# Sign-carrying weight decode by Prelu, and one-hot steps and float16 copies on GpSimd, in a clustered attention and MLP kernel

## The chip, the cores and the metric

The kernel runs on 1 core of one Trainium2 chip. The metric is the device time of one execution in microseconds. TensorE is written PE in the profile, VectorE DVE, ScalarE ACT, GpSimd POOL and the engine whose queue issues the DMAs SP.

## The reference, cut to what matters

Queries and keys are assigned to the nearest of 16 centroids of their head; a query attends only to keys of its own cluster; the result goes through a two-layer MLP with a squared ReLU. All inputs come as float64.

```python
q_assign = np.argmax(np.einsum('bhsd,hcd->bhsc', q_n, c_n), axis=-1)
k_assign = np.argmax(np.einsum('bhsd,hcd->bhsc', k_n, c_n), axis=-1)
mask = q_assign[:, :, :, None] == k_assign[:, :, None, :]
scores = scale * np.matmul(q, k.transpose(0, 1, 3, 2))
scores = np.where(mask, scores, -1000000000.0)
attn = softmax(scores);  x = (attn @ v) as 3072 x 512
h = x @ w_in;  r = np.maximum(h, 0.0);  g = s * (r * r) + b
out = (g @ w_out).astype(np.float32)
```

The shapes are batch 4, 8 heads, 768 positions, head size 64; `w_in` is 512 x 2048, `w_out` 2048 x 512.

## The kernel before, in words

**Attention.** The work is cut into 192 units, one for each batch `b`, third of the sequence `c`, pair of heads `hp`, tile of 128 rows `t` and head of the pair `h`. For a unit, `scores` (L447) makes four products on TensorE: two of the data halves (KA, QA) and two of the halves that hold the mask (KB, QB). `maxima` (L461) takes the row maximum on VectorE (L465), `exps` (L467) the exponential on ScalarE (L475) into a float32 tile `p`. From unit `RAW = 8` on, `high` (L480) makes a float16 copy `ph` of `p`, and `low` (L487) subtracts it on GpSimd (L498), so that two float16 halves stand for one float32; one DMA transpose issued by SP (L500) turns both into `PT`. `values` (L502) multiplies with V. The first 8 units are turned on TensorE instead (L495). In `high` the copy is ScalarE's, but for the odd units from 17 to 35, which are VectorE's.

**Masks.** `prep_k` (L301) and `prep_q` (L332 on) prepare a pair of heads of K and four heads of Q for later units, in steps spread over the loop. Each ends in `onehot` (L283): from the products with the centroids in PSUM, VectorE takes the maximum (L288), compares (L289), multiplies with a falling row `rev` so that the first of equal maxima wins (L291), takes the maximum again (L292), compares (L293) and writes the result four times side by side as 0 and 32768 or their negatives (L294). A DMA transpose on SP's queue (L392 for `QB`, L342 for `KB`) turns it; the second pair of `scores` of the units that use it waits for that. Eight units share one `QB`. There are 16 K preparations and 24 Q preparations.

**Weights.** `fetch` (L189) loads 32 tiles (16 of each matrix), 512 KB of float64 each, into a `stage` pool of three buffers. A float64 is decoded into a float32 by hand. `rebase` (L201) reads the high 32-bit word as a float32: ScalarE multiplies it by 2^-112 (L203) and writes its sign as bf16 into `wsg` (L205). `narrow` (L207) shifts left by 3 (L209) and ors in the top three bits of the low word (L210), both on VectorE; the shift throws the sign away. `bound` (L213) gathers magnitudes: for `w_out` tiles ScalarE takes the absolute value with a running sum (L216), for `w_in` tiles TensorE adds the high halves of the words through a matrix of ones (L221) and VectorE takes the maximum (L222). GpSimd then multiplies the sign back (L223). When all are decoded, `wsplit` (L261) scales each tile into a float16 pair (L267 on ScalarE, L269 on VectorE).

**MLP.** 192 steps (12 row blocks, 16 slices of the hidden width). Step m stands `LAG = 21` units behind unit m: `mlp_in` (L575), ReLU and squares on ScalarE (L582 to L585), a subtraction on GpSimd (L590), `mlp_out` (L602).

**Order.** The loop at L700 writes the steps of unit i, MLP step i - 21, the preparations and two pieces of the weights' generator into one program. The framework then orders each engine's instructions by a timeline of its own at build time (L757, `schedule_with_timeline_sim=True`), after the priorities that `first_of_all` gives. On the chip each engine and SP's queue work strictly in the order that results.

## Time and profile before

| | |
|---|---|
| time, median of 3 runs | 986.11 us (985.94 to 988.25) |
| span of the profiled execution | 986.0 us |
| VectorE busy | 673.0 us (68%) |
| ScalarE busy | 726.4 us (74%) |
| GpSimd busy | 550.2 us (56%) |
| TensorE busy | 834.3 us (85%) |

The profile gives no other time of the profiled execution than its span, from the first instruction to the last; it stands 0.1 us from the median. Busy time is the time in which at least one instruction of an engine runs. A row of a group gives the line, the engine, the operation, output and inputs with their shapes, the count, the busy time, the mean of one in ns, and the idle time before them with what ended it. A row of the windows gives a stretch of the span, then the busy time and count of each engine, the granted clock of TensorE, the busy share of the DMA engines and the rate in GB/s.

### The profile page before, as it was taken

How to read it: one execution, taken by the hardware profiler on the slowest of the kernel's cores; microseconds unless marked ns; L12 is line 12 of the kernel's file. 1: busy time of each engine (PE TensorE's matmuls, PEld its weight loads, DVE VectorE, ACT ScalarE, POOL GpSimd, SP SyncE). 2: the span in 40 equal slices, each digit the busy share in tenths (PEclk: the TensorE clock that was granted, in tenths of full speed). 3: DMA queues.
4: the chain of work that ended last, by engine and by line, in shares of the span. 5: the costliest groups of instructions: out<-in, count | busy, mean ns of one | idle time of the engine just before them, and what ended most of it. 6: DMA issues, size and time to landing. Idle time of an engine off the chain costs nothing. (4 is left out here: it accounts for less than half of the span.)

```text
span 986.0 us, 22497 instructions
## 1 busy us (share of the span) xinstructions
PE 834.3 (85%) x8625; PEld 580.2 (59%) x8625; DVE 673.0 (68%) x1475; ACT 726.4 (74%) x1416; POOL 550.2 (56%) x543
## 2 busy tenths in 40 slices
PE   0568524887899999998799999997889999999997
PEld 0347312654566666765566666765666666767764
DVE  7798889989687665658787756578867567473100
ACT  4476776877578788867678877876788977789443
POOL 3125755556456576655467656655566766667322
PEclk9955566999999999999999999999999999999999
DMA  6865883687678775698888767797888676777200
GB/s 181 204 196 158 222 210 90 138 194 134 128 144 163 156 161 123 140 210 154 171 164 156 169 132 156 138 203 181 138 160 173 151 119 142 142 138 149 44 23 21
DMA packets 450299, 147.36 MB, mean 149 GB/s; under 512 B 417936, under 2 KB 446608, under 8 KB 450192
## 3 DMA queue, kind: packets, MB, share of 16 engines
q1 hardware_dynamic: 450192, 145.93, 69.7%
q8 instruction: 67, 1.10, 0.5%
q14 instruction: 40, 0.33, 0.1%
HBM read 35.69 MB, written 6.29 MB: 43 GB/s over the span
## 5 line engine op out<-in xcount | busy, mean ns | idle before, releaser
L498 POOL TENSOR_TENSOR ph<-p,ph 128x768 f16<-128x768 f32 x184 | 308.6, 1677 | 170.7 <-ACT ph L119 135.8
L575 PE MATMUL h<-x,wis 128*128 128x256 f16 x2304 | 292.0, 275 | 17.3 <-ACT r L582 12.2
L602 PE MATMUL acc<-wos,g 128*128 128x512 f16 x1152 | 295.4, 380 | 4.7 <-POOL g L590 2.9
L575 PEld LDWEIGHTS <-wis 128*128 128x128 f16 x2304 | 223.1, 98 | 74.9 <-issue 16.6
L590 POOL TENSOR_TENSOR g<-r,g 128x256 f16<-128x256 f32 x192 | 133.3, 695 | 139.7 <-ACT r L585 129.8
L465 DVE TENSOR_REDUCE ssm<-sc 128x1 f32<-128x768 f32 x192 | 180.9, 950 | 16.2 <-PE sc L456 16.0
L475 ACT ACTIVATE p<-sc,ssm,qsm 128x768 f32<-128x768 f32 x192 | 188.1, 980 | 3.9 <-DMA PT<-ph 1.8
L602 PEld LDWEIGHTS <-g 128*128 128x128 f16 x1152 | 104.1, 98 | 88.2 <-POOL g L590 6.9
L119 ACT ACTIVATE ph<-p 128x768 f16<-128x768 f32 x174 | 144.8, 832 | 11.1 <-DMA PT<-ph 10.8
L472 ACT ACTIVATE ssm<-ssm,lift,qsm 128x1 f32<-128x1 f32 x192 | 73.4, 382 | 101.9 <-DVE ssm L465 101.4
L517 PE MATMUL px<-vh,PT 128*128 128x65 f16 x1104 | 119.9, 196 | 14.5 <-DVE ksm L98 5.2
L582 ACT ACTIVATE r<-h,cf 128x256 f32<-128x256 f32 x192 | 89.1, 464 | 55.0 <-PE h L575 50.8
L518 PE MATMUL px<-vl,PT 128*128 128x64 f16 x1104 | 119.9, 193 | 0.0
L519 PE MATMUL px<-vh,PT 128*128 128x65 f16 x1104 | 119.9, 194 | 0.0
L456 PE MATMUL sc<-KA,QA 128*128 128x384 f16 x384 | 101.1, 343 | 20.2 <-ACT p L475 16.9
L518 PEld LDWEIGHTS <-PT 128*128 128x128 f16 x1104 | 103.6, 100 | 21.2 <-issue 12.8
L517 PEld LDWEIGHTS <-PT 128*128 128x128 f16 x1104 | 103.9, 98 | 17.5 <-issue 9.1
L456 PE MATMUL sc<-KB,QB 128*128 128x384 f16 x384 | 100.2, 345 | 7.8 <-DMA QB<-qb 7.7
L519 PEld LDWEIGHTS <-PT 128*128 128x128 f16 x1104 | 103.6, 98 | 3.0
L584 ACT ACTIVATE g<-r 128x256 f16<-128x256 f32 x192 | 79.5, 414 | 3.8
L585 ACT ACTIVATE r<-r 128x256 f32<-128x256 f32 x192 | 79.1, 412 | 3.3
L525 DVE TENSOR_SCALAR ssm<-px 128x2 f32<-128x2 f32 x92 | 14.2, 155 | 88.3 <-PE px L519 88.2
(153 smaller groups left out, 1090.9 us busy)
## 6 DMA issues: line engine op xcount, KB each, us to landing
wst<-in_moe_w_in_dram SPq DMA_DIRECT2D x16, 512.0 KB, 4.5
wst<-in_moe_w_out_dram SPq DMA_DIRECT2D x16, 512.0 KB, 4.1
kn<-in_k_dram SPq DMA_DIRECT2D x16, 384.0 KB, 3.9
qn<-in_q_dram SPq DMA_DIRECT2D x24, 256.0 KB, 3.8
vn<-in_v_dram SPq DMA_DIRECT2D x16, 384.0 KB, 4.4
out_dram<-o SPq DMA_DIRECT2D x12, 512.0 KB, 3.2
PT<-ph SPq DMA_TRANSPOSE x184, 3.4
x<-xn SPq DMA_TRANSPOSE x48, 2.5
```

Of the source, the lines that this page charges most:

```text
L119: A.activation(dst, src, AF.Copy)
L456: last_score[0] = nc.tensor.matmul(sc[:, e, :HALF], X[:, col, :], y[:, h * S + e * HALF : h * S + (e + 1) * HALF], start=st, stop=not st)
L465: last_max[0] = V.tensor_reduce(SM[i // 4][:, 0, j : j + 1], U[i]["sc"], axis=AX.XY, op=ALU.max, negate=True)
L475: last_exp[0] = A.activation(p.rearrange("p (a b) -> p a b", a=2), u["sc"], AF.Exp, bias=bi, scale=u["scale"], **total)
L498: G.tensor_tensor(u["ph"][:, 1, :], u["p"], u["ph"][:, 0, :], op=ALU.subtract)
L517: nc.tensor.matmul(o1, PT[:, kt, :], vh[:, h, kt, : D + 1], start=(kt == 0), stop=False)
L518: nc.tensor.matmul(o, PT[:, kt, :], vl[:, h, kt, :], start=False, stop=False)
L519: nc.tensor.matmul(o1, PT[:, T + kt, :], vh[:, h, kt, : D + 1], start=False, stop=(kt == T - 1))
L575: nc.tensor.matmul(ph[:, :CW], WSP[ft][0][:, wl, kt, :], XS[(b, c, kt)][:, :, xl, :], start=(i == 0), stop=(i == len(terms) - 1))
L582: A.activation(r, ph[:, :CW], AF.Relu, scale=MS[(b, c)][0])
L590: G.tensor_tensor(g[:, 1, :], r, g[:, 0, :], op=ALU.subtract)
L602: nc.tensor.matmul(acc[:, t, :], g[:, gl, rows], WSP[ft][1][:, wl, :], start=(ft == 0 and gl + wl == 0), stop=(ft == NF - 1 and gl == 1))
```

## The change

Three things change.

1. `rebase` makes one ScalarE pass with Prelu instead of two. A positive word is scaled by 2^-112 as before; a negative one is multiplied by 2^-112 and by -2^32, so that after the shift by 3 the bit that becomes the sign is set. `wsg` and GpSimd's multiplication by it are gone. Because the decoded word is now signed, `bound` writes absolute values to a bf16 tile `wab` for both matrices: the `w_out` tiles as before with the running sum, the `w_in` tiles by a pass that is new, and TensorE reads `wab`.
2. In `onehot`, the steps L291 and L294 are GpSimd's, but for the first two K preparations and the first Q preparation. The four other steps stay VectorE's.
3. `high` gives the float16 copies of units 8 to 18 to GpSimd (`LAG - 2 = 19`; units below 8 make none). Before, unit 17 was VectorE's and the others ScalarE's. From unit 19 on nothing changes.

```diff
 def rebase(d):
     hw = d["st"][:, :, :, 1].bitcast(F32)
-    A.activation(d["w"], hw, AF.Copy, scale=2.0 ** -112)
-    d["sg"] = sb.tile([P, KT, P], BF16, tag="wsg", name=f"wsg_{d['p']}", bufs=2)
-    A.activation(d["sg"], hw, AF.Sign)
+    A.activation(d["w"], hw, AF.Prelu, scale=2.0 ** -112, alpha=-(2.0 ** 32))
...
 def bound(d):
     w, p, ft = d["w"], d["p"], d["ft"]
+    wa = sb.tile([P, KT, P], BF16, tag="wab", name=f"wab_{p}", bufs=2)
     if p % 2:
-        A.activation(w, w, AF.Abs, accum_out=l1[:, ft : ft + 1])
+        A.activation(wa, w, AF.Abs, accum_out=l1[:, ft : ft + 1])
     else:
-        wa = w.bitcast(BF16).rearrange("p a (f z) -> p a f z", z=2)[:, :, :, 1]
+        A.activation(wa, w, AF.Abs)
         pw = ps_h.tile([P, 512], F32, tag="h", name=f"pw_{ft}")
         for t in range(KT):
             nc.tensor.matmul(pw[:, :P], ones, wa[:, t, :], start=(t == 0), stop=(t == KT - 1))
         V.tensor_reduce(w1[:, ft : ft + 1], pw[:, :P], axis=AX.X, op=ALU.max)
-    G.tensor_tensor(w, w, d["sg"], op=ALU.mult)
...
-def onehot(pa, nb, name, dst, mul, add):
+def onehot(pa, nb, name, dst, mul, add, eng):
...
-    V.tensor_tensor(e, e, rev.unsqueeze(1).broadcast_to([P, nb, C]), op=ALU.mult)
+    eng.tensor_tensor(e, e, rev.unsqueeze(1).broadcast_to([P, nb, C]), op=ALU.mult)
     V.tensor_reduce(m, e, axis=AX.X, op=ALU.max)
     V.tensor_tensor(o, e, m.unsqueeze(2).broadcast_to([P, nb, C]), op=ALU.is_equal)
-    V.tensor_scalar(dst, o.unsqueeze(2).broadcast_to([P, nb, 4, C]), mul, add, op0=ALU.mult, op1=ALU.add)
+    eng.tensor_scalar(dst, o.unsqueeze(2).broadcast_to([P, nb, 4, C]), mul, add, op0=ALU.mult, op1=ALU.add)
...
-    yield from onehot(pa, 2 * T, f"k{n}", mk, BIG, -BIG)
+    yield from onehot(pa, 2 * T, f"k{n}", mk, BIG, -BIG, G if b or hp > 1 else V)
...
-    yield from onehot(pa, nh * CT, f"q{n}", mk, BIG, 0.0)
+    yield from onehot(pa, nh * CT, f"q{n}", mk, BIG, 0.0, G if b or c or hq else V)
...
-    copy(V if LAG - 4 <= i < LAG + NF and i % 2 else A, u["ph"][:, 0, :], u["p"])
+    copy(G if i < LAG - 2 else V if i < LAG + NF and i % 2 else A, u["ph"][:, 0, :], u["p"])
```

The lines behind `rebase` have smaller numbers in the changed kernel (L498 becomes L496, L291 becomes L289); this text keeps the numbers of the kernel before. The order of the instructions moves in many places, since the framework lays it out anew. Three of them follow.

GpSimd in the middle of the weights' decode, around unit 10 (`ph_10` is its float16 pair, `wi8` and `wo8` decoded tiles, `xn` the normalised output of the attention, `oe_q` and `qb` the one-hot of a Q preparation), before:

```order
L223 TENSOR_TENSOR wi8_814<-wi8_814,wsg_16_878 128x512
L498 TENSOR_TENSOR ph_10_1061<-p_10_1016,ph_10_1061 128x768
L543 TENSOR_TENSOR xn_1_1088<-xs_1_969,xn_1_1088 128x2x128
L223 TENSOR_TENSOR wo8_872<-wo8_872,wsg_17_923 128x512
L498 TENSOR_TENSOR ph_11_1121<-p_11_1065,ph_11_1121 128x768
L223 TENSOR_TENSOR wi9_882<-wi9_882,wsg_18_933 128x512
L223 TENSOR_TENSOR wo9_927<-wo9_927,wsg_19_990 128x512
L498 TENSOR_TENSOR ph_12_1190<-p_12_1126,ph_12_1190 128x768
```

GpSimd at the same units, now:

```order
L121 CAST ph_10_1026<-p_10_984 128x768
L541 TENSOR_TENSOR xn_1_1053<-xs_1_940,xn_1_1053 128x2x128
L496 TENSOR_TENSOR ph_10_1026<-p_10_984,ph_10_1026 128x768
L121 CAST ph_11_1083<-p_11_1030 128x768
L289 TENSOR_TENSOR oe_q0_1_0_1115<-oe_q0_1_0_1115,rev_73 128x128
L496 TENSOR_TENSOR ph_11_1083<-p_11_1030,ph_11_1083 128x768
L121 CAST ph_12_1149<-p_12_1088 128x768
L292 TENSOR_SCALAR qb_0_1_0_950<-oo_q0_1_0_1116 128x8x64
L496 TENSOR_TENSOR ph_12_1149<-p_12_1088,ph_12_1149 128x768
```

The products with the sign are gone from between the subtractions; a copy stands ahead of each subtraction, and the two steps of a one-hot stand between them.

ScalarE at the end of the decode (`wst` are staged tiles, `wi15` and `wo15` the last decoded ones, `wis0` and `wos0` the first scaled ones, `p_18` the exponential of unit 18), before:

```order
L203 ACTIVATE wo15_1299<-wst_31_1300 128x512
L205 ACTIVATE wsg_31_1384<-wst_31_1300 128x512
L216 ACTIVATE wo15_1299,l1_129<-wo15_1299 128x512
L267 ACTIVATE wis0_1488<-wi0_256,glob_130 128x512
L267 ACTIVATE wos0_1511<-wo0_259,glob_130 128x512
L185 ACTIVATE qb_0_1_1_1485<-qn_0_1_1_1285,qsm_0_1_1_1363 128x4x64 x2
L475 ACTIVATE p_18_1499<-sc_18_1490,ssm_16_1408,qsm_0_1_0_852 128x768
```

ScalarE at the same place, now:

```order
L203 ACTIVATE wo15_1254<-wst_31_1255 128x512
L470 ACTIVATE ssm_16_1360<-ssm_16_1360,lift_132,qsm_0_1_0_829 128x1
L473 ACTIVATE p_16_1363<-sc_16_1353,ssm_16_1360,qsm_0_1_0_829 128x768
L215 ACTIVATE wab_31_1340,l1_129<-wo15_1254 128x512
L265 ACTIVATE wis0_1440<-wi0_256,glob_130 128x512
L470 ACTIVATE ssm_16_1360<-ssm_16_1360,lift_132,qsm_0_1_0_829 128x1
L473 ACTIVATE p_17_1384<-sc_17_1375,ssm_16_1360,qsm_0_1_0_829 128x768
L265 ACTIVATE wos0_1463<-wo0_259,glob_130 128x512
```

The sign pass is gone, and the last tile is decoded and the first scaled while unit 17 is still to come; before, the next exponential behind them was unit 18's. The decode ends one unit earlier in the order of the units.

GpSimd around unit 60, where a Q preparation (`q1_1_0`, used from unit 64 on) is under way (`g` are the MLP's float16 halves), before:

```order
L590 TENSOR_TENSOR g_0_2_5_4573<-r_0_2_5_4571,g_0_2_5_4573 128x256
L498 TENSOR_TENSOR ph_60_4744<-p_60_4684,ph_60_4744 128x768
L590 TENSOR_TENSOR g_0_2_6_4618<-r_0_2_6_4616,g_0_2_6_4618 128x256
L498 TENSOR_TENSOR ph_61_4829<-p_61_4748,ph_61_4829 128x768
L590 TENSOR_TENSOR g_0_2_7_4701<-r_0_2_7_4699,g_0_2_7_4701 128x256
L498 TENSOR_TENSOR ph_62_4870<-p_62_4833,ph_62_4870 128x768
```

GpSimd there, now:

```order
L588 TENSOR_TENSOR g_0_2_5_4525<-r_0_2_5_4523,g_0_2_5_4525 128x256
L496 TENSOR_TENSOR ph_60_4696<-p_60_4636,ph_60_4696 128x768
L289 TENSOR_TENSOR oe_q1_1_0_4678<-oe_q1_1_0_4678,rev_73 128x128
L588 TENSOR_TENSOR g_0_2_6_4570<-r_0_2_6_4568,g_0_2_6_4570 128x256
L496 TENSOR_TENSOR ph_61_4781<-p_61_4700,ph_61_4781 128x768
L292 TENSOR_SCALAR qb_1_1_0_4490<-oo_q1_1_0_4679 128x8x64
L588 TENSOR_TENSOR g_0_2_7_4653<-r_0_2_7_4651,g_0_2_7_4653 128x256
```

The one-hot's two steps stand in GpSimd's queue behind the subtractions of units 60 and 61; the transpose of `QB` is behind the second of them.

## The prediction

> **What bounds the kernel now.** I read the windows of the span first, because the kernel has stages with different limits. Each row is a stretch, then busy time and count of PE, PEld, DVE, ACT and POOL, PE's granted clock, the DMA share and GB/s.
>
> ```profile
> 45.00:157.00 112.00, 59.23 (x385) 43.02 (x383) 96.86 (x174) 79.63 (x153) 55.89 (x43) 0.60 0.72 197
> 157.00:200.00 43.00, 33.61 (x392) 23.45 (x391) 40.90 (x91) 33.72 (x65) 25.44 (x21) 0.85 0.53 116
> 200.00:260.00 60.00, 48.49 (x464) 30.38 (x462) 54.13 (x115) 45.96 (x85) 35.10 (x29) 0.94 0.85 164
> 260.00:915.00 655.00, 613.82 (x6757) 430.26 (x6756) 440.10 (x979) 516.63 (x1009) 404.04 (x383) 1.00 0.76 154
> ```
>
> The first row is the decode of 29 or 30 of the 32 weight tiles: DVE is busy 96.9 of 112 us (86%), ACT 71%, PE 53% at a clock of 0.60. DVE sets the pace. From 157 to 260 the weights are scaled; DVE is busy 95.0 of 103 us and still ahead of PE (82.1). From 260 on PE is busy 613.8 of 655 us (94%): there a faster DVE buys only what is left of PE's 41 us of idle time.
>
> Next, the groups of the decode stage alone, for DVE and for POOL.
>
> ```profile
> L210 DVE SCALAR_TENSOR_TENSOR wo<-wst,wo 128x512 uint32<-128x512 uint32 x15 | 17.7, 1179 | 0.2
> L209 DVE TENSOR_SCALAR wo<-wo 128x512 int32<-128x512 int32 x15 | 13.4, 895 | 2.9 <-ACT wo L203 2.9
> L210 DVE SCALAR_TENSOR_TENSOR wi<-wst,wi 128x512 uint32<-128x512 uint32 x14 | 11.5, 824 | 0.2
> L209 DVE TENSOR_SCALAR wi<-wi 128x512 int32<-128x512 int32 x14 | 7.8, 559 | 3.7 <-ACT wi L203 3.7
> ```
>
> ```profile
> L223 POOL TENSOR_TENSOR wi<-wi,wsg 128x512 f32<-128x512 f32 x15 | 18.9, 1262 | 30.9 <-PE pw L221 14.6 <-ACT ssm L472 13.5 <-DVE xs L529 2.7
> L223 POOL TENSOR_TENSOR wo<-wo,wsg 128x512 f32<-128x512 f32 x15 | 18.7, 1249 | 20.9 <-ACT wo L216 16.1 <-DVE wi L210 2.6 <-ACT wsg L205 2.1
> L498 POOL TENSOR_TENSOR ph<-p,ph 128x768 f16<-128x768 f32 x9 | 15.8, 1756 | 7.0 <-ACT ph L119 7.0
> ```
>
> The same DVE instruction on the same shape has means of 559 and 895 ns, or 824 and 1179 ns. The timeline shows why: start, duration, engine and operation.
>
> ```profile
> 140.47 0.94 DVE L465 TENSOR_REDUCE ssm<-sc 128x1 f32<-128x768 f32 x1
> ...
> 141.33 0.41 DVE L209 TENSOR_SCALAR wi<-wi 128x512 int32<-128x512 int32 x1
> 141.38 1.38 POOL L223 TENSOR_TENSOR wo<-wo,wsg 128x512 f32<-128x512 f32 x1 [1.38 <-ACT wo L216]
> 141.78 1.53 DVE L210 SCALAR_TENSOR_TENSOR wi<-wst,wi 128x512 uint32<-128x512 uint32 x1
> ...
> 144.08 1.15 POOL L223 TENSOR_TENSOR wi<-wi,wsg 128x512 f32<-128x512 f32 x1 [1.32 <-PE pw L221]
> 144.29 1.22 DVE L209 TENSOR_SCALAR wo<-wo 128x512 int32<-128x512 int32 x1
> 145.55 0.69 DVE L210 SCALAR_TENSOR_TENSOR wo<-wst,wo 128x512 uint32<-128x512 uint32 x1
> ```
>
> Beside a sign product on POOL the shift took 1.22 us instead of 0.41 and the or 1.53 instead of 0.69: each ended only after POOL's instruction had. So POOL's work in this stage is paid by the engine that bounds it.
>
> **The change part by part.** The sum is made against the span of 986.0 us, 0.1 us from the median of 986.11.
>
> *The sign product goes.* L209 and L210 together took 17.7 + 13.4 + 11.5 + 7.8 = 50.4 us in the stage. Undisturbed, 29 tiles would take 29 x (0.41 + 0.69) = 31.9. The excess is 18.5 us for 55.9 us of POOL work, 0.33 us of DVE for each us of POOL. L223 is 37.6 of those, so its share is 12.4 us.
>
> *New POOL work in the stage.* Nine copies now stand ahead of the nine subtractions, and four one-hots (two K, two Q) bring two steps each. The trace has no POOL copy from float32 to float16 of this size, no product of 128 or 192 columns and no tensor-scalar. The nearest rows are of the whole span:
>
> ```profile
> L590 POOL TENSOR_TENSOR g<-r,g 128x256 f16<-128x256 f32 x192 | 133.3, 695 | 139.7 <-ACT r L585 129.8 <-DMA PT<-ph 4.5 <-issue 3.8
> L375 POOL COPY qa<-qb 128x512 f16<-128x512 f16 x24 | 18.0, 750 | 0.0
> L325 POOL COPY kb<-ka 128x768 f16<-128x768 f16 x16 | 15.7, 982 | 32.9 <-DMA KB<-kb 23.9 <-ACT ka L185 8.9
> ```
>
> For the copy I take the 0.98 us of L325, with the same 768 columns; the ends are 0.75 (L375) and 1.76 (L498). For L291 on POOL I take 0.5, between nothing and the 0.70 of L590, which is twice as wide; for L294 I take 0.75 (Q) and 0.98 (K) from L375 and L325, the upper end again 1.76. That makes 8.8 us of copies and 4 x 0.5 + 2 x 0.75 + 2 x 0.98 = 5.5 us of one-hots, 14.3 in all. At 0.33 they cost DVE 4.7 us; the ends are 2.5 and, if DVE pays every us, 14.3.
>
> *The steps that leave DVE.* Their rows, of the whole span:
>
> ```profile
> L291 DVE TENSOR_TENSOR oe_q<-oe_q,rev 128x128 f32<-128x128 f32 x24 | 20.4, 849 | 0.5
> L294 DVE TENSOR_SCALAR qb<-oo_q 128x512 f16<-128x512 f16 x24 | 16.3, 678 | 0.4
> L294 DVE TENSOR_SCALAR kb<-oo_k 128x768 f16<-128x768 f16 x16 | 8.9, 558 | 0.3
> L291 DVE TENSOR_TENSOR oe_k<-oe_k,rev 128x192 f32<-128x192 f32 x16 | 7.3, 455 | 0.3
> ```
>
> In the decode, 2 x (0.85 + 0.68) + 2 x (0.46 + 0.56) = 5.1 us leave. But DVE's second maximum (L292) must now wait for POOL, and DVE's whole queue behind it: row maxima, shifts and ors. That costs between nothing (the order puts other DVE work between) and one L498 (1.76 us) each; I take 0.5, 2 us in all.
>
> *DVE in the decode:* -12.4 + 4.7 - 5.1 + 2 = -10.8 us. At 86% busy that is worth 9.3 us, if nothing else is late next. Something may be: the loads.
>
> ```profile
> 105.00:120.00 15.00, 6.50 (x70) 4.19 (x69) 11.38 (x21) 11.12 (x21) 9.46 (x8) 0.61 1.04 267
> 120.00:135.00 15.00, 5.28 (x51) 3.47 (x50) 12.78 (x16) 9.84 (x19) 9.26 (x8) 0.61 0.81 209
> 135.00:150.00 15.00, 4.28 (x20) 2.33 (x20) 13.92 (x17) 9.90 (x19) 8.62 (x7) 0.61 0.90 240
> ```
>
> From 105 to 150 us the DMA engines are busy 92%, so these 45 us can shrink by 3.7 at the very most; I count half, 1.9. The other 67 us get 67/112 of 9.3, 5.6. The decode ends 7.5 us earlier.
>
> *ScalarE.* One row each for the passes concerned, whole span:
>
> ```profile
> L119 ACT ACTIVATE ph<-p 128x768 f16<-128x768 f32 x174 | 144.8, 832 | 11.1 <-DMA PT<-ph 10.8 <-POOL ph L498 0.2
> ...
> L205 ACT ACTIVATE wsg<-wst 128x512 bf16<-128x512 f32 x32 | 21.0, 655 | 7.2 <-POOL wo L223 4.5 <-POOL wi L223 2.6
> ...
> L203 ACT ACTIVATE wi<-wst 128x512 f32<-128x512 f32 x16 | 10.6, 659 | 7.0 <-DMA wst<-in_moe_w_in_dram 7.0
> L216 ACT ACTIVATE wo<-wo 128x512 f32<-128x512 f32 x16 | 10.0, 626 | 11.4 <-DVE wo L210 11.3
> ```
>
> ACT loses 32 signs (21.0 us) and 10 copies (8.3) and gets 16 magnitudes (10.0): 19.3 us less. I take Prelu at the 0.66 of the scaled copy, since Sign on the same shape takes that too; a pass as long as two would cost 21 us. ACT is at 71% in the decode, so this counts as nothing, covered by DVE. Were ACT the bound instead, the 19.3 us would count in full.
>
> *PE's magnitudes.* L221 now waits for ACT's pass behind L210, and the scores in PE's queue wait with it. In the same stage PE waited already:
>
> ```profile
> PE pw L221 <- DVE wi L210: 27.2, 7, 5.9
> ```
>
> The pass adds 0.63 us to each of 16, 10 us of PE waiting. PE is 53% busy there, so I count nothing, with 10 as the other end.
>
> *157 to 260.* Three Q one-hots and one K leave DVE: 3 x 1.53 + 1.0 = 5.6 us; waits and contention return about 3 as above. I take -2. *Order:* the decode ends one unit earlier in the sequence, so that unit falls to the stretch where PE is full; it costs between nothing and all PE work per unit and step, 834.3/192 = 4.3 us:
>
> ```profile
> PE 834.3 (85%) x8625; PEld 580.2 (59%) x8625; DVE 673.0 (68%) x1475; ACT 726.4 (74%) x1416; POOL 550.2 (56%) x543
> ```
>
> I take 2, since the step's half of that work is needed either way. *From 260 on:* nothing, with bounds below.
>
> Sum: -7.5 - 2 + 2 = -7.5, which gives **978.5 us**.
>
> *A rule against the row.* The Trainium skill, SBUF — State Buffer, section "Who interferes with whom", says that VectorE and GpSimd share one port pair, locked whole for an instruction, and that a reduction never contends. The pairs above agree, and the L465 reduction ahead of them took 0.94 us. By that rule POOL would cost DVE its share of lockable instructions, at least 50.4/96.9 = 0.52 per us rather than 0.33; as an estimate, the net of the first two terms would be (37.6 - 14.3) x 0.52 = 12.1 us instead of 7.7, and the sum about 975.
>
> **The rivals.** *The one-hot gets late (slower).* From 260 us on 18 Q preparations pass through POOL twice. What waits there now:
>
> ```profile
> PE sc L456 <- ACT p L475: 6.0, 6, 1.8
> PE sc L456 <- DMA QB<-qb: 5.8, 7, 2.0
> PE px L517 <- DVE ksm L98: 3.7, 3, 1.7
> ```
>
> ```profile
> POOL ph L498 <- ACT ph L119: 128.6, 92, 6.4
> ```
>
> PE waits for `QB` in 7 cases already, so these have no slack. The order of POOL puts a subtraction between the one-hot's two steps; it waits 1.4 us on the mean for ACT (128.6/92), and itself takes up to 1.76. `QB` would come 1.4 to 3.2 us later; SP's queue holds the transposes of later `ph` and the loads behind it too. Seven times 2.3 are 16 us on PE: 986 - 7.5 + 16 = 994.5. It decides from 7.5/7 = 1.1 us per case. For it speaks that POOL is 62% busy there, against it that all these waits sum to 5.8 us now and that the new order can place other products ahead. The Trainium skill's GPSIMD Engine Reference, section "4.1 Engine selection", says the same as a rule: elementwise work belongs on VectorE, GpSimd being about half as fast with two inputs.
>
> *DMA or PE takes DVE's place.* If loads hold the late decode fully and PE's clock of 0.60 the early one, 1 to 3 us stay: 984.5. The 92% speak for it; the early part, where DMA has room, against.
>
> *DVE's relief reaches PE.* The 29 remaining one-hots (18 Q, 11 K) free up to 1.5 us of DVE each after 260; if half of the QB, p and ksm waits and as much of the other idle time among the 41 us goes, 10 us come on top: 968.5. DVE's 33% of idle time there speaks against.
>
> **How the numbers follow.** The forecast has 0.53, late one-hots 0.17, DMA or PE in DVE's place 0.17, full relief 0.13. A measurement can tell 0.3%, about 3 us, from no change. The forecast and the full relief lie on the faster side, 0.66; DMA or PE in place gives 0.17 of no change, late one-hots 0.17 slower. The range reaches below the full relief, to 965, by the copy's low end and the lock's rule, and up to 991, part of the way to late one-hots; it leaves out most of their 0.17.
>
> **What would show it.** Right: L209 and L210 near 0.5 and 0.8 us in the decode, its last L210 7 us earlier, POOL's copies near 1 us, the PE idle time after 260 near 41 us. Wrong: waits of PE for `QB` above 15 us; DVE waiting for POOL at L292 by more than 1 us each; DMA at 1.0 through the decode with its end unmoved.

## The result, and the profile after

The changed kernel takes 958.91 us (median of 4 runs, 956.34 to 961.42); the kernel before took 986.66 us beside it (median of 4 runs, 985.94 to 988.25). The ratio is 0.9709, with a 95% interval from 0.9682 to 0.9735: 28 us faster, nearly four times the 7.5 us that were forecast, and below the low end of the range. The profiled execution has a span of 957.6 us (its own time is 959.63), 28.4 us less than the span before.

The totals by engine (busy time, share of the span, instructions) of the kernel after:

```profile
PE 831.2 (87%) x8625; PEld 580.0 (61%) x8625; DVE 614.9 (64%) x1400; ACT 709.9 (74%) x1390; POOL 568.9 (59%) x596
```

VectorE lost 58 us, ScalarE 16.5, GpSimd gained 19, and TensorE's work is the same. Where the 28.4 us lie is read from three landmarks in VectorE's timeline: the last or of the decode, the first output tile `o` of the MLP and the 21st. Before:

```profile
153.65 1.44 DVE L210 SCALAR_TENSOR_TENSOR wo<-wst,wo 128x512 uint32<-128x512 uint32 x1
...
268.57 1.41 DVE L610 SCALAR_TENSOR_TENSOR o<-acc,xm,bias 128x512 f32<-128x512 f32 x2
...
939.65 1.41 DVE L610 SCALAR_TENSOR_TENSOR o<-acc,xm,bias 128x512 f32<-128x512 f32 x2 [8.69 <-PE acc L602]
```

After (the lines behind `rebase` have lost two in their numbers, or one):

```profile
131.54 0.69 DVE L208 SCALAR_TENSOR_TENSOR wo<-wst,wo 128x512 uint32<-128x512 uint32 x1
...
245.67 1.41 DVE L608 SCALAR_TENSOR_TENSOR o<-acc,xm,bias 128x512 f32<-128x512 f32 x2
...
911.19 1.41 DVE L608 SCALAR_TENSOR_TENSOR o<-acc,xm,bias 128x512 f32<-128x512 f32 x2 [6.09 <-PE acc L600]
```

The decode ends at 132.2 instead of 155.1 us: 22.9 us earlier. From there to the first output tile both kernels take 113.5 us. From the first to the 21st it is 665.5 us instead of 671.1, 5.6 us less; the 46.4 us behind it are unchanged. 22.9 + 0 + 5.6 is the 28.4 up to rounding.

The windows of the decode, before and after (columns as in the prediction: stretch, PE, PEld, DVE, ACT, POOL, clock, DMA share, GB/s):

```profile
45.00:155.10 110.10, 58.71 (x382) 42.78 (x380) 95.39 (x164) 78.23 (x150) 54.80 (x42) 0.60 0.73 200
```

```profile
45.00:132.20 87.20, 52.34 (x366) 40.20 (x367) 75.98 (x155) 60.77 (x122) 30.79 (x28) 0.62 0.90 236
```

VectorE is busy 19.4 us less and idle 3.5 us less (11.2 instead of 14.7). The DMA engines carry nearly the same loads, 0.73 x 110.1 = 80.4 us of full share before and 0.90 x 87.2 = 78.5 after, in less time: their share went up. The shift and the or after, in that stage:

```profile
L208 DVE SCALAR_TENSOR_TENSOR wi<-wst,wi 128x512 uint32<-128x512 uint32 x14 | 15.5, 1106 | 0.1
...
L208 DVE SCALAR_TENSOR_TENSOR wo<-wst,wo 128x512 uint32<-128x512 uint32 x15 | 12.8, 851 | 0.1
L207 DVE TENSOR_SCALAR wi<-wi 128x512 int32<-128x512 int32 x14 | 8.1, 577 | 4.4 <-ACT wi L203 4.4
L207 DVE TENSOR_SCALAR wo<-wo 128x512 int32<-128x512 int32 x15 | 6.8, 453 | 3.7 <-ACT wo L203 3.7
```

They sum to 43.2 us instead of 50.4. The `wo` tiles gained; the ors on `wi` tiles got worse (15.5 instead of 11.5): GpSimd's subtractions and copies still run beside some of them (one took 2.15 us at 121.85 us, beside a subtraction that began at 121.82). GpSimd's new work in the same stage:

```profile
L121 POOL CAST ph<-p 128x768 f16<-128x768 f32 x8 | 8.7, 1082 | 16.5 <-ACT p L473 14.4 <-issue 2.1
...
L292 POOL TENSOR_SCALAR kb<-oo_k 128x768 f16<-128x768 f16 x2 | 1.7, 832 | 7.2 <-DVE vm L60 3.7 <-DVE oo_k L291 3.6
L292 POOL TENSOR_SCALAR qb<-oo_q 128x512 f16<-128x512 f16 x2 | 1.6, 804 | 4.3 <-DVE oo_q L291 4.3
L289 POOL TENSOR_TENSOR oe_k<-oe_k,rev 128x192 f32<-128x192 f32 x2 | 1.2, 592 | 27.8 <-DVE oe_k L287 21.6 <-DVE amb_v L413 6.2
L289 POOL TENSOR_TENSOR oe_q<-oe_q,rev 128x128 f32<-128x128 f32 x2 | 0.9, 456 | 2.6 <-DVE oe_q L287 2.6
```

These durations are close to those taken from neighbouring rows (0.98 for the copy, 0.5, 0.98 and 0.75 for the others).

In the steady part, the window after:

```profile
260.00:915.00 655.00, 620.36 (x6779) 435.19 (x6780) 398.45 (x916) 519.29 (x1015) 440.05 (x443) 0.99 0.76 152
```

VectorE is busy 398 us instead of 440, and TensorE 620.4 instead of 613.8. What TensorE still waits for there (the wait, total, times, longest), after:

```profile
PE pk L336 <- DVE cf L562: 5.8, 2, 3.3
PE pk L336 <- DVE xs L527: 5.1, 2, 3.8
...
PE h L573 <- ACT r L580: 3.1, 6, 0.9
PE sc L454 <- DMA QB<-qb: 3.0, 4, 1.5
PE sc L454 <- ACT p L473: 2.7, 6, 0.6
```

Before, in the same stretch:

```profile
PE h L575 <- ACT r L582: 12.2, 10, 3.1
PE sc L456 <- ACT p L475: 6.0, 6, 1.8
PE sc L456 <- DMA QB<-qb: 5.8, 7, 2.0
```

The waits for ScalarE's `r` and `p` fell from 18.2 to 5.8 us, and the waits for `QB` fell too. Part of this returned as waits for VectorE (`cf`, `xs`).

### The profile page after: what moved, and what is told of

It reads as the page before. It is cut to its first block, busy times and chain, and to the rows that moved or that the text cites. A ratio compares the mean times of both kernels' runs of the same rounds, so it can differ in the third digit from the quotient of the medians.

```text
span 957.6 us, 22486 instructions
## 1 busy us (share of the span) xinstructions
PE 831.2 (87%) x8625; PEld 580.0 (61%) x8625; DVE 614.9 (64%) x1400; ACT 709.9 (74%) x1390; POOL 568.9 (59%) x596
## 5 line engine op out<-in xcount | busy, mean ns | idle before, releaser
L496 POOL TENSOR_TENSOR ph<-p,ph 128x768 f16<-128x768 f32 x184 | 314.2, 1707 | 123.7 <-ACT ph L119 82.7
L600 PE MATMUL acc<-wos,g 128*128 128x512 f16 x1152 | 298.5, 381 | 5.0 <-POOL g L588 4.6
L119 ACT ACTIVATE ph<-p 128x768 f16<-128x768 f32 x164 | 136.3, 831 | 9.1 <-DMA PT<-ph 8.7
L515 PE MATMUL px<-vh,PT 128*128 128x65 f16 x1104 | 119.6, 196 | 10.8 <-DVE xs L527 4.6
L454 PE MATMUL sc<-KA,QA 128*128 128x384 f16 x384 | 99.8, 342 | 20.4 <-ACT p L473 17.4
L523 DVE TENSOR_SCALAR ssm<-px 128x2 f32<-128x2 f32 x92 | 14.3, 155 | 79.9 <-PE px L517 79.8
```

The source lines that it names most:

```text
L119: A.activation(dst, src, AF.Copy)
L454: last_score[0] = nc.tensor.matmul(sc[:, e, :HALF], X[:, col, :], y[:, h * S + e * HALF : h * S + (e + 1) * HALF], start=st, stop=not st)
L496: G.tensor_tensor(u["ph"][:, 1, :], u["p"], u["ph"][:, 0, :], op=ALU.subtract)
L515: nc.tensor.matmul(o1, PT[:, kt, :], vh[:, h, kt, : D + 1], start=(kt == 0), stop=False)
L600: nc.tensor.matmul(acc[:, t, :], g[:, gl, rows], WSP[ft][1][:, wl, :], start=(ft == 0 and gl + wl == 0), stop=(ft == NF - 1 and gl == 1))
```

## The experiments

Ratios are to the kernel before, run on the same chip, with the 95% interval. Microseconds made from a ratio are the ratio times 986.66. The other columns are from the profiled execution of each kernel: the end of the decode, VectorE's busy and idle time from 45 us to there, the time from there to the first output tile, and from the first to the 21st.

| kernel | ratio | decode end | VectorE busy, idle | to first `o` | first to 21st |
|---|---|---|---|---|---|
| before | 1 | 155.1 | 95.4, 14.7 | 113.5 | 671.1 |
| after | 0.9709 [0.9682, 0.9735] | 132.2 | 76.0, 11.2 | 113.5 | 665.5 |
| prelu_alone | 0.9851 [0.9823, 0.988] | 139.4 | 74.2, 20.2 | 118.0 | 668.3 |
| onehot_alone | 0.98 [0.9758, 0.9842] | 146.9 | 90.8, 11.1 | 111.2 | 659.6 |
| copies_back | 0.9722 [0.9677, 0.9766] | 135.0 | 73.1, 16.9 | 113.9 | 663.2 |
| onehot_back | 0.9886 [0.9856, 0.9917] | 142.2 | 77.9, 19.3 | 115.8 | 669.0 |
| pool_product_kept | 0.992 [0.9892, 0.9949] | 146.7 | 85.1, 16.6 | 122.5 | 664.5 |
| act_sign_kept | 0.9765 [0.9731, 0.9799] | 138.1 | 74.8, 18.3 | 113.6 | 665.7 |
| act_pass_off_stage | 0.9739 [0.9712, 0.9766] | 136.7 | 75.4, 16.3 | 115.4 | 663.9 |
| onehot_first_batch | 0.9788 [0.9756, 0.9819] | 130.7 | 75.6, 10.1 | 116.4 | 668.9 |
| startup_onehots_back | 0.976 [0.973, 0.979] | 139.6 | 75.5, 19.1 | 114.9 | 661.8 |
| startup_onehots_alone | 0.9942 [0.9918, 0.9966] | 147.5 | 90.5, 12.0 | 116.8 | 671.5 |
| before_q01_ahead | 0.9987 [0.997, 1.0003] | 148.7 | 90.8, 12.9 | 115.1 | 676.6 |
| after_q01_ahead | 0.9688 [0.965, 0.9726] | 134.9 | 74.8, 15.1 | 115.0 | 662.5 |
| startup_q01_ahead | 0.9747 [0.9715, 0.9779] | 138.8 | 75.7, 18.1 | 117.1 | 661.7 |
| onehot_q01_ahead | 0.9871 [0.984, 0.9903] | 138.5 | 76.2, 17.3 | 119.8 | 668.9 |
| prelu_q01_ahead | 0.9824 [0.9797, 0.9852] | 136.5 | 74.4, 17.1 | 111.0 | 671.0 |

The number of units whose maxima are done when the decode ends is 18 to 20, so a unit more or less (0.95 us of VectorE for the maximum alone) lies in each of these numbers. Every edit makes the framework lay out the whole program anew; differences of 2 or 3 us between two layouts are not read as causes.

### The parts alone and undone

**prelu_alone**: the kernel before with the first part only (shortened; the lines of `bound` for `wab` are as in the change).

```diff
-    A.activation(d["w"], hw, AF.Copy, scale=2.0 ** -112)
-    d["sg"] = sb.tile([P, KT, P], BF16, tag="wsg", name=f"wsg_{d['p']}", bufs=2)
-    A.activation(d["sg"], hw, AF.Sign)
+    A.activation(d["w"], hw, AF.Prelu, scale=2.0 ** -112, alpha=-(2.0 ** 32))
...
-    G.tensor_tensor(w, w, d["sg"], op=ALU.mult)
```

> Only the Prelu decode of the change; the one-hot steps and the float16 copies as before. Theory A (GpSimd's sign products slowed VectorE, which bounds the decode): most of the 22 us by which the decode's end came earlier, 12 to 17, so 970 to 975 us, with L209 near 0.45 and L210 near 0.8 us in the decode. Theory B (what counted was ScalarE's time: 19 us less of it, 8 of them by the copies): about 8 to 11 us, 976 to 979. Theory C (the one-hot steps that left VectorE carried it): under 5 us, above 981.

**onehot_alone**: the kernel before with the second part only (shortened; `onehot` itself is as in the change).

```diff
-    yield from onehot(pa, 2 * T, f"k{n}", mk, BIG, -BIG)
+    yield from onehot(pa, 2 * T, f"k{n}", mk, BIG, -BIG, G if b or hp > 1 else V)
...
-    yield from onehot(pa, nh * CT, f"q{n}", mk, BIG, 0.0)
+    yield from onehot(pa, nh * CT, f"q{n}", mk, BIG, 0.0, G if b or c or hq else V)
```

> Only the one-hot steps on GpSimd; the decode with signs and the copies as before. Theory A: 5 us of VectorE time leave the decode and as much the stage behind it, but GpSimd's queue is filled by the sign products there: 3 to 8 us gained, 979 to 984. Theory C: the decode ends 12 us earlier or more, under 975. The rival of the prediction (late masks hold TensorE): above 990.

**copies_back**: the kernel after with the float16 copies where they were.

```diff
-    copy(G if i < LAG - 2 else V if i < LAG + NF and i % 2 else A, u["ph"][:, 0, :], u["p"])
+    copy(V if LAG - 4 <= i < LAG + NF and i % 2 else A, u["ph"][:, 0, :], u["p"])
```

> The changed kernel with the float16 copies of units 8 to 18 back on ScalarE and VectorE; Prelu and the one-hots stay. In the decode GpSimd loses some 8.7 us and ScalarE gets 7.5. Theory A (VectorE's time, about 0.3 us for each us of GpSimd): 2 to 3 us of VectorE less, 955 to 959 us. Theory B (ScalarE's time counts too, as the sign pass that was put back showed with 6 us for 14): 3 us more, 960 to 963.

**onehot_back**: the kernel after with all one-hot steps on VectorE.

```diff
-    yield from onehot(pa, 2 * T, f"k{n}", mk, BIG, -BIG, G if b or hp > 1 else V)
+    yield from onehot(pa, 2 * T, f"k{n}", mk, BIG, -BIG, V)
...
-    yield from onehot(pa, nh * CT, f"q{n}", mk, BIG, 0.0, G if b or c or hq else V)
+    yield from onehot(pa, nh * CT, f"q{n}", mk, BIG, 0.0, V)
```

> The changed kernel with all one-hot steps back on VectorE; Prelu and the copies on GpSimd stay. If the parts add up: the decode ends 4 to 6 us later, and the stretch behind it, from the first output on, takes 3 to 6 us longer: 966 to 971. If the one-hots only help where the sign products still burden VectorE: 958 to 962.

The parts form a chain: before to prelu_alone is 0.0149 of the time (14.7 us), prelu_alone to copies_back, which has Prelu and the one-hots, another 0.0129 (12.7 us), and the copies the last 0.0013 (1.3 us), which can't be told from nothing. In the other order the one-hots come first with 19.7 us and Prelu then brings 7.7: the two overlap by some 7 us. Taken from the kernel after, the one-hots are worth 0.0177, 17.5 us. The forecast had given the one-hots about 3 us in all (5.1 in the decode less waits and contention, and 2 behind it). They are the larger surprise; Prelu's part was also too small.

Against what was expected of these four: prelu_alone fell where its theory A had it (972 us). onehot_alone, at 967 us, was 12 us below its theory A, and its decode ended 8.2 us earlier, not the 12 of its theory C. onehot_back, at 975 us, lies above both of its ranges. copies_back (959 us) doesn't decide between its two.

The traces of the chain also part the shift and the or. In prelu_alone's decode they took:

```profile
L208 DVE SCALAR_TENSOR_TENSOR wo<-wst,wo 128x512 uint32<-128x512 uint32 x15 | 13.0, 868 | 0.2
L208 DVE SCALAR_TENSOR_TENSOR wi<-wst,wi 128x512 uint32<-128x512 uint32 x14 | 10.9, 782 | 0.2
L207 DVE TENSOR_SCALAR wo<-wo 128x512 int32<-128x512 int32 x15 | 6.3, 422 | 10.2 <-ACT wo L203 10.2
L207 DVE TENSOR_SCALAR wi<-wi 128x512 int32<-128x512 int32 x14 | 5.9, 423 | 5.0 <-ACT wi L203 5.0
```

That is 36.1 us instead of the 50.4 before, 14.3 less for 36.5 us of GpSimd work less: 0.39 us for each. In copies_back, with the one-hots, they took 36.8, and in the kernel after, with the copies too, 43.2. So the copies gave back 6.4 us on these lines, though the total doesn't show it.

### Which side of the Prelu part pays

**pool_product_kept**: the kernel after, with a product of the same shape put back on GpSimd at the old place. Its result goes, as bf16, to a scratch tile that nothing reads.

```diff
+    scr = sb.tile([P, KT, P], BF16, tag="wsx", name=f"wsx_{p}", bufs=1)
+    G.tensor_tensor(scr, w, ones.unsqueeze(1).broadcast_to([P, KT, P]), op=ALU.mult)
```

> The changed kernel, and GpSimd makes a product of each decoded tile again, into a scratch tile that nobody reads, so that only its time and its place on GpSimd return. Theory A: 33 us and more of GpSimd time in the decode cost VectorE about a third of it and more as in the kernel before, the time rises by 8 to 14 us to 967 to 973. Theory B and C: nothing waits for the product, the time stays within 3 us of 959, and GpSimd's queue in the decode has room for it.

It costs 0.0211, 20.8 us, though nothing reads its result: more than the whole Prelu part gained. Its window of the decode:

```profile
45.00:146.70 101.70, 56.47 (x393) 41.69 (x392) 85.09 (x163) 62.93 (x126) 61.66 (x55) 0.62 0.74 208
```

GpSimd is busy 30.9 us more than in the kernel after, VectorE 9.1 us more: 0.29 us for each us of GpSimd, over the whole of VectorE. This isn't the 0.33 of the prediction, which was the shift's and the or's alone: those sum to 44.6 us here, only 1.4 more than in the kernel after. Some 4.6 us lie in other instructions that took longer (passes over V and Q and the small scale steps), and some 3 in instructions that fall into the longer stage. So VectorE pays for GpSimd's time, but not at one rate, and that isn't the whole price. The decode is 14.5 us longer (VectorE's idle time grew by 5.4 as well, its wait for scores from 0.8 to 6.8), and the way to the first output tile 9 us more. The copies, the one-hots and the subtractions stand behind the products in GpSimd's queue; the row maximum of unit 8, whose `QB` GpSimd helps to make, ends at 82.1 us instead of 72.2. How the rest divides was not separated, and the 8 to 14 us that theory A expected were too few. The timelines of GpSimd and VectorE in this kernel show that instructions of two elements pay as well as large ones (start, duration):

```profile
88.11 1.54 POOL L223 TENSOR_TENSOR wsx<-wi,ones 128x512 bf16<-128x512 f32 x1 [1.63 <-DVE qsm L69]
89.73 1.16 POOL L223 TENSOR_TENSOR wsx<-wo,ones 128x512 bf16<-128x512 f32 x1
```

```profile
88.56 1.11 DVE L70 TENSOR_SCALAR qsm<-qsm 128x2 f32<-128x2 f32 x1
89.71 0.16 DVE L362 TENSOR_TENSOR qsm<-qsm,ksm 128x2 f32<-128x2 f32 x1
89.90 1.00 DVE L363 TENSOR_TENSOR qsm<-qsm,ksm 128x2 f32<-128x2 f32 x1
90.94 0.17 DVE L64 TENSOR_SCALAR qsm<-qsm 128x2 int32<-128x2 int32 x1
```

Two instructions on 128 x 2 elements took 1.11 and 1.00 us beside a product and ended 0.02 and 0.01 us after it; their neighbours took 0.16 and 0.17.

**act_sign_kept**: the kernel after with ScalarE's sign pass put back; its result isn't read.

```diff
+    sg = sb.tile([P, KT, P], BF16, tag="wsg", name=f"wsg_{d['p']}", bufs=1)
+    A.activation(sg, hw, AF.Sign)
```

> The changed kernel, and ScalarE makes the sign pass again, into a tile that nobody reads; the stage buffer is free only after it. 21 us of ScalarE time return. Theory A: ScalarE is not the bound, 0 to 4 us more, 959 to 963. Theory B: the load, decode, free loop of three buffers and ScalarE's queue set the pace, 8 to 15 us more, 967 to 974.

**act_pass_off_stage**: the same pass, but in `bound` and on the decoded tile, so that it doesn't hold the staged tile.

```diff
+    sg = sb.tile([P, KT, P], BF16, tag="wsg", name=f"wsg_{p}", bufs=1)
+    A.activation(sg, w, AF.Sign)
```

> The changed kernel, and ScalarE makes a sign pass again, into a tile that nobody reads, but from the decoded tile: ScalarE's time returns, and the stage buffer is not held longer. If the 6 us that the sign pass on the stage cost were ScalarE's time: 963 to 967. If they were the buffer's longer hold: 957 to 960.

The passes took 18.9 us of ScalarE's time in the decode in the first kernel and 17.4 in the second, and cost 5.5 and 3.0 us of the total: 964 and 961 us, each between the two ranges that were expected of it. With the intervals of both kernels combined (root of the sum of squares), the first difference is clear of noise (0.0056 against 0.0043) and the second isn't (0.0030 against 0.0038). In the first the row maximum of unit 8 ends at 87.2 us instead of 72.2, in the second at 72.5; so the 5.5 us can be the held staged tile and a late unit as well as ScalarE's time. ScalarE's relief is small, and which of these it works by is open.

### Where the one-hots pay

**onehot_first_batch**: the kernel after, with only the one-hots of the first batch on GpSimd; the 12 K and 18 Q preparations of the later batches go back to VectorE.

```diff
-    yield from onehot(pa, 2 * T, f"k{n}", mk, BIG, -BIG, G if b or hp > 1 else V)
+    yield from onehot(pa, 2 * T, f"k{n}", mk, BIG, -BIG, G if b == 0 and hp > 1 else V)
...
-    yield from onehot(pa, nh * CT, f"q{n}", mk, BIG, 0.0, G if b or c or hq else V)
+    yield from onehot(pa, nh * CT, f"q{n}", mk, BIG, 0.0, G if b == 0 and c + hq else V)
```

> The changed kernel, but of the one-hots only those of batch 0 are GpSimd's; the 12 K and 18 Q preparations of the later batches are VectorE's again. The decode should end as in the changed kernel, at 132 us. If VectorE's relief reached TensorE behind it: from the first to the eleventh pair of outputs 670 us again instead of 665.5, 962 to 967 in all. If that difference was chance of the order: 956 to 961. If the path through GpSimd made masks late: under 956.

It costs 0.0079, 7.8 us. That makes 966 us, in the range that was expected if VectorE's relief reaches TensorE. The decode is not longer, so what is lost lies behind it. (Its profiled execution, 3.8 us below its median, shows 4.7 us of it: 2.9 up to the first output tile and 3.4 from there to the 21st, less 1.5 in the decode.) The wait that tells is ScalarE's for the row maxima, from 260 to 915 us; in this kernel, before, and after:

```profile
ACT ssm L470 <- DVE ssm L463: 77.6, 67, 4.0
```

```profile
ACT ssm L472 <- DVE ssm L465: 83.8, 70, 4.3
```

```profile
ACT ssm L470 <- DVE ssm L463: 51.9, 58, 2.8
```

With the later one-hots on VectorE (this kernel, before, and prelu_alone with 77.9) the exponentials wait 78 to 84 us for maxima; with them on GpSimd (after, copies_back 49.5, onehot_alone 50.8) some 50. In the same two groups TensorE's wait for `r` is 11.2 to 12.7 us against 3.1 to 3.7, and it is busy 614 to 616 of the 655 us against 620 to 624. The last column of the table parts the same way, without overlap: 659.6 to 665.7 us in the nine kernels that have the later one-hots on GpSimd, 668.3 to 676.6 in the eight that have them on VectorE. One place in the kernel before shows how (start, duration):

```profile
814.34 0.49 PE L456 MATMUL sc<-KB,QB 128*128 128x384 f16 x2
...
814.85 1.74 DVE L294 TENSOR_SCALAR qb<-oo_q 128x512 f16<-128x512 f16 x1
...
816.52 1.81 DVE L465 TENSOR_REDUCE ssm<-sc 128x1 f32<-128x768 f32 x2
...
817.50 0.39 ACT L472 ACTIVATE ssm<-ssm,lift,qsm 128x1 f32<-128x1 f32 x1 [2.51 <-DVE ssm L465]
```

The score products end at 814.83. The two row maxima start only behind the one-hot's last step, which takes 1.74 us here (a subtraction runs on GpSimd from 814.80 to 816.44), and ScalarE waits 2.51 us for the first maximum. So the row maxima stood behind the one-hot steps in VectorE's queue and ScalarE behind the maxima; that TensorE stood behind ScalarE is read from its waits for `r`.

**startup_onehots_back**: the kernel after, with the third and fourth K and the second Q preparation (which are made while the decode runs) back on VectorE.

```diff
-    yield from onehot(pa, 2 * T, f"k{n}", mk, BIG, -BIG, G if b or hp > 1 else V)
+    yield from onehot(pa, 2 * T, f"k{n}", mk, BIG, -BIG, G if b else V)
...
-    yield from onehot(pa, nh * CT, f"q{n}", mk, BIG, 0.0, G if b or c or hq else V)
+    yield from onehot(pa, nh * CT, f"q{n}", mk, BIG, 0.0, G if b or c else V)
```

> The changed kernel with only three one-hots back on VectorE: those of the K preparations 2 and 3 and of the second Q preparation of the first block, which the units from 8 on need. Theory D (these three were late behind VectorE's queue, and the row of units stood still between unit 7 and unit 8 for 26 us in the kernel before, 14 in the changed one): unit 8's maximum ends near 90 us instead of 72, the decode ends 6 to 10 us later, 966 to 970 in all. Theory A alone (VectorE's time): three one-hots are 3 to 4 us, 960 to 964.

**startup_onehots_alone**: the kernel before with just these three on GpSimd (shortened; `onehot` itself is as in the change).

```diff
-    yield from onehot(pa, 2 * T, f"k{n}", mk, BIG, -BIG)
+    yield from onehot(pa, 2 * T, f"k{n}", mk, BIG, -BIG, G if not b and hp > 1 else V)
...
-    yield from onehot(pa, nh * CT, f"q{n}", mk, BIG, 0.0)
+    yield from onehot(pa, nh * CT, f"q{n}", mk, BIG, 0.0, G if not b and not c and hq else V)
```

> The kernel before with only those three one-hots on GpSimd. Theory D: unit 8's maximum ends near 76 us instead of 89, the decode ends 6 to 9 us earlier, 977 to 981. Theory A alone: 3 to 4 us, 982 to 985.

Three preparations, six instructions of 0.46 to 0.99 us on GpSimd in the kernel after, are worth 5.0 us when they are undone (0.0051, where the two intervals combined are 0.0040) and 5.7 when done alone. Undone, VectorE's busy time in the decode is the same as after (75.5 against 76.0): the gain is in its idle time, 19.1 us against 11.2. Done alone, both fall, busy time from 95.4 to 90.5 and idle time from 14.7 to 12.0. By the end of the decode (7.4 us later and 7.6 us earlier) theory D was right; by the time, the first lies in theory A's range and the second at the upper end of theory D's. These 5.0 us and the 7.8 of the later batches make 12.8 of the 17.5 that all the one-hots are worth; the other four Q preparations of the first batch were not tested alone. In every kernel up to here that has them on VectorE the second `QB` comes late: the row maximum of unit 8, the first unit that needs it, ends near 92 us instead of 72 when Prelu is there (88.8 in the kernel before). That became the next theory.

### Is it the place of the second `QB` in the order?

**before_q01_ahead** and **after_q01_ahead**: the second Q preparation is written ahead of the fourth K preparation, in the kernel before and in the one after.

```diff
             if k == 2:
-                run(first_k[3])
+                run(first_q[1])
                 some(first_v, 1)
             if k == 3:
-                run(first_q[1])
+                run(first_k[3])
```

> The kernel before, in which the second Q preparation of the first block is finished one unit earlier in the program and K preparation 3, needed only from unit 12 on, one later; no work moves between engines. Theory D: unit 8's maximum ends 5 to 12 us earlier and the decode 3 to 8 us, 978 to 983. Theory A alone: no engine gets less work, within 2 us of 987.

> The same exchange of the two preparations in the changed kernel. Theory D: unit 8 starts 3 to 6 us earlier still and the time falls by 1 to 4 us, 955 to 958. Where the DMA engines, busy 0.9 in its decode, now set the pace: within 2 us of 959.

**startup_q01_ahead**, **onehot_q01_ahead** and **prelu_q01_ahead**: the same edit in startup_onehots_back, onehot_back and prelu_alone. They keep the steps on VectorE and move only the place.

> The changed kernel with the three start-up one-hots on VectorE and the second Q preparation built ahead of the fourth K preparation. In SP's order the transpose of the second QB then stands behind 12 loads of weight tiles instead of 17, as it does in the changed kernel. Theory (the start-up one-hots pay by the place of that transpose, and not by VectorE's time): the row maximum of unit 8 comes near 75 us instead of 92, the DMA share from 75 to 105 us rises above 0.8, the decode ends near 134 us instead of 139.6, and the time goes from 0.976 to about 0.971 of the kernel before. Rival (VectorE's time on these steps is what counts): unit 8 moves, but the decode's end and the time stay within 2 us of 139.6 and 0.976.

> The changed kernel with all one-hot steps on VectorE and the same swap. Theory: unit 8 near 75 us instead of 92, the decode ends near 135 us instead of 142.2, and 6 to 8 us of the 18 that the one-hots are worth come back: about 0.981 of the kernel before instead of 0.9886; the rest is lost from 250 us on, where TensorE's idle time stays near 39 us. Rival: 0.9886 within 0.003, as the swap alone did nothing in the kernel before.

> The kernel before with the decode by one Prelu alone and the same swap; one-hots and copies as before. Theory: unit 8 near 75 us instead of 92, the dip of the DMA share from 75 to 105 us (0.67 and 0.59) fills up, the decode ends near 133 us instead of 139.4, and the time is about 0.979 of the kernel before instead of 0.9851. Rival: 0.9851 within 0.003.

Unit 8 moved in all of them (maxima ended at 79 us in the kernel before with this edit, 72.7 to 74.3 in the last three), but the totals hardly did: 1.3, 1.5 and 2.7 us less than without the edit, each within the overlap of the intervals, and nothing in the kernel before, although its decode ended 6.4 us earlier (the stretch from the first to the 21st output tile took 5.5 us more). The last three lie in time where their rivals had them, and in startup_q01_ahead the decode ends at 138.8 us, where the theory had 134 and its rival 139.6. The theory that the start-up one-hots pay by the place of `QB` falls. after_q01_ahead (956 us) doesn't decide between what was expected of it. What is different still is in SP's queue. In startup_q01_ahead:

```profile
72.69 0.53 SPq L85 DMA_DIRECT2D qn<-in_q_dram  x1
79.75 1.19 SPq L544 DMA_TRANSPOSE x<-xn  x1
81.03 0.53 SPq L85 DMA_DIRECT2D wst<-in_moe_w_in_dram  x1
```

In the kernel after:

```profile
69.60 0.43 SPq L85 DMA_DIRECT2D qn<-in_q_dram  x1
73.87 0.37 SPq L85 DMA_DIRECT2D wst<-in_moe_w_in_dram  x1
74.78 1.20 SPq L544 DMA_TRANSPOSE x<-xn  x1
```

In the first the queue stands 6.5 us at the transpose of the first `x`, which waits for GpSimd's `xn`, and three loads issue behind it in a row, of which the first is shown; in the second a load stands ahead of it and the transpose waits 0.5 us. In all the kernels that have the Prelu and the start-up steps on VectorE this wait is 5.7 to 6.5 us, and the DMA share from 75 to 105 us is 0.63 to 0.87 instead of 0.90. Against it as the only cause stands after_q01_ahead, which waits 5.0 us there and is as fast as the kernel after. No kernel that moves this transpose alone was run, so this part of the gain, some 5 us, is placed (in VectorE's idle time of the decode) and not explained.

The fastest of all is after_q01_ahead with 0.9688; its interval overlaps with that of the kernel after, so it is not shown to be faster.

## Why the prediction was wrong

The direction and the mechanism were right: GpSimd's time in the decode is paid by VectorE, whose busy time there fell by 21.2 us in prelu_alone and grew by 9.1 in pool_product_kept. The size was wrong by 20.9 us of span, of which 15.4 lie in the decode and 5.6 from the first output tile on. By its steps:

**The sign product and the new work on GpSimd.** -12.4 and +4.7, together -7.7 us for the shift and the or; measured -7.2. Right as a sum, and in part by luck: taken alone the Prelu part gave 14.3 us, not 12.4, and the copies took back 6.4, where 8.8 us at 0.33 are 2.9. The rate isn't one number: these two lines paid 0.39 us for each us of GpSimd in prelu_alone and 0.05 in pool_product_kept (1.4 of 30.9). By the rule of the Trainium skill, SBUF — State Buffer, section "Who interferes with whom", the estimate was 0.52, over the whole of VectorE. The runs don't decide for it or against it: VectorE's busy time changed by 0.58 us for each us of GpSimd in prelu_alone and by 0.29 in pool_product_kept. The reduction that the prediction set beside that rule had no product beside it (GpSimd's began 0.03 us before it ended); the 16 row maxima of the decode, some of them beside products, all took 0.94 to 0.96 us.

**The one-hots that leave the decode.** -5.1; measured -6.1 (in the kernel before L291 and L294 took 1.7 + 1.1 + 2.6 + 0.7 us there). Right.

**Waits at L292.** +2; none is among VectorE's waits in the decode. From 260 us on there are 12 for Q of 1.0 us on the mean and 8 for K of 0.9; the move gained there all the same.

**VectorE's sum, -10.8.** Too small: busy time fell 19.4 us. The working priced GpSimd's disturbance on two lines alone. Other lines paid as well. Before:

```profile
L293 DVE TENSOR_TENSOR oo_q<-oe_q,om_q 128x128 f16<-128x128 f32 x2 | 1.8, 877 | 0.0
...
L293 DVE TENSOR_TENSOR oo_k<-oe_k,om_k 128x192 f16<-128x192 f32 x2 | 1.6, 795 | 0.0
```

After:

```profile
L291 DVE TENSOR_TENSOR oo_k<-oe_k,om_k 128x192 f16<-128x192 f32 x2 | 0.7, 338 | 0.0
...
L291 DVE TENSOR_TENSOR oo_q<-oe_q,om_q 128x128 f16<-128x128 f32 x2 | 0.6, 284 | 0.0
```

The comparisons of the one-hots, the small scale steps (L69's one instruction went from 1.07 to 0.16 us) and a pass over Q give about 4 us; two units fewer in the stage give 1.9 (L465); the rest is the -7.2 and -6.1.

**86% of it, capped by the loads.** "These 45 us can shrink by 3.7 at the very most; I count half": this step failed plainly. It took the loads of 105 to 150 us as tied to that stretch. The windows of the decode in thirds show what they did, before:

```profile
45.00:75.00 30.00, 20.24 (x135) 14.86 (x134) 27.93 (x61) 22.65 (x47) 6.77 (x5) 0.65 0.70 217
75.00:105.00 30.00, 21.82 (x108) 17.62 (x106) 25.36 (x48) 21.64 (x43) 18.24 (x15) 0.56 0.59 151
```

After:

```profile
45.00:75.00 30.00, 20.30 (x144) 15.71 (x144) 28.23 (x67) 23.44 (x49) 4.96 (x7) 0.72 0.83 238
75.00:105.00 30.00, 20.96 (x118) 17.16 (x118) 24.69 (x50) 21.38 (x44) 10.90 (x9) 0.59 0.90 232
105.00:132.20 27.20, 11.08 (x107) 7.34 (x106) 23.06 (x40) 15.95 (x30) 14.92 (x12) 0.56 0.97 238
```

A load issues when a staged tile comes free; SP's queue waits for VectorE's or, L208, before it (31.4 us of such waits in the decode after). Tiles came free sooner from 45 us on, and loads moved into a part that had 0.59 of the DMA engines busy. The cap has to be taken over the whole stage: 110.1 - 80.4 = 29.7 us, of which 22.9 were used. Nor was the factor of 86% right: idle time fell along with busy time. The rival that loads take VectorE's place came true in this sense only: at 0.90 they are now close behind.

**ScalarE, nothing.** A pass put back cost 5.5 us in act_sign_kept and 3.0 in act_pass_off_stage, of which the first alone is clear of noise: small, but not shown to be nothing. **TensorE's magnitudes, nothing**: its wait for VectorE's or (27.2 us) became one of 7.5 us for ScalarE's `wab`; what the pass costs was not measured alone.

**157 to 260 and the order, -2 and +2.** Together nothing; measured nothing (113.5 us both times). The two were not measured apart, and the same stretch takes 111.0 to 122.5 us in the other kernels, so this agreement may be luck.

**From 260 on, nothing.** Wrong: -5.6 us. This was the third rival, VectorE's relief reaching TensorE, with a chance of 0.13. What spoke against it, 33% of idle time on VectorE, does not bear on it: an engine in strict order that is idle a third of the time still delays a row maximum by the one-hot step ahead of it (1.74 us in the rows at 814.85 us). onehot_first_batch puts this relief at 7.8 us of the total, 4.7 in its profiled execution.

**The late one-hot.** It didn't come: the waits for `QB` fell from 5.8 to 3.0 us. The rule of the Trainium skill, GPSIMD Engine Reference, section "4.1 Engine selection", that elementwise work belongs on VectorE, is not borne out for this place. GpSimd is slower, as the rule has it: a step takes 0.5 to 0.8 us there, the K steps left on VectorE take 0.36. The move still gains 12.7 to 19.7 us, since it is VectorE's queue that others wait for.

Of the signs that the prediction named for itself, the shift at 0.51 us and the copies at 1.08 came true; the or took 0.98 instead of 0.8, the decode ended 22.9 us earlier instead of 7, and TensorE's idle time after 260 us was 34.6 instead of 41.

So the step to name is the end of the decode's sum. The terms on single lines were right within 1 us as they were added up; what failed was the passage from them to the stage and from the stage to the steady part. Of the 15.4 us missing in the decode, 8.6 are VectorE's sum, which took two lines for a whole engine (-19.4 instead of -10.8), 3.3 the factor of 86% with the cap on part of the stage (which made 7.5 of 10.8), and 3.5 the idle time that fell as well. The steady part, put at nothing, is the other 5.6.

## What to carry to other kernels

When a contending engine is relieved, price every instruction that runs beside it, the tiny ones too, and not only the two longest lines; and expect what stands behind it in its own queue to cost as well. Take the cap of a second resource over the whole stretch in which its work can move, here 29.7 us rather than 3.7. And in a part where another engine is 94% busy, look for what stands ahead of that engine's suppliers in a strict queue: idle time of the engine that owns the queue doesn't excuse it.

## What the runs showed of the hardware

GpSimd products whose results nobody reads, 33.5 us of them in the decode, cost 20.8 us of the total. VectorE instructions on 128 x 2 elements took 1.0 to 1.1 us beside such a product, to its end, instead of 0.15 to 0.17. A Prelu pass over 128 x 512 with a slope of -2^32 takes what the scaled copy took, 0.66 to 0.67 us. GpSimd's float32 to float16 copy of 128 x 768 took 1.08 us on the mean in the decode, 0.25 us more than ScalarE's 0.83.
